# Scoring two neighbouring chunks back to back in batches 2 and 3 of a woven attention and MLP kernel

## The chip, the cores and the metric

The kernel runs on one core of a Trainium2 chip. The metric is the device time of one execution in microseconds (us), the median of several executions. TensorE is called PE here, VectorE DVE, ScalarE ACT, GpSimd POOL and SyncE SP, as the profile calls them.

## The reference, cut to what matters

Four batches, 8 heads, 768 positions, head size 64. A decaying linear attention, then a low-rank mixer over positions, then a two-layer MLP:

```python
for t in range(S):                      # attention, per batch and head
    state = gamma * state + outer(k[t], v[t])
    y[t] = scale * q[t] @ state
x = heads side by side of y             # (4, 768, 512)
u = x + (x.T @ U @ V).T                 # rank 32
out = u + relu(u @ w_ch1) @ w_ch2       # 512 -> 2048 -> 512
```

The kernel cuts the 768 positions into six chunks of 128. Within a chunk the attention is a masked score matrix (**score**, q times k, then **masking**), applied to v and added to q times the carried state (**mix**); **state** carries on to the next chunk.

## The kernel before: the parts that matter

PE works through the MLP of batch b-1, cut into pieces, and the attention of batch b is woven in between at marks, given as shares of that MLP's work. So "batch 2" below is the stretch in which the attention of batch 2 lies among the MLP pieces of batch 1. PSUM has eight banks, dealt out in rings:

```python
RINGS = {"mlp": [0, 1, 2], "s": [3, 4], "o": [5], "qk": [6], "st": [7],
         "A": [6, 0], "B": [1], "C": [2]}
...                                     # from batch 2 on: RINGS["mlp"] = [6, 0, 1, 2]

def score(b, ci):
    kT, qT = live["k", b, ci // 2][:, ci % 2], q_cols(b, ci)
    sp = [bank("s") for _ in range(2)]
    for h in range(H):                  # 8 matmuls of 64 rows
        r = ds(D * (h % 2), D)
        nc.tensor.matmul(sp[h % 2][:, ts(h // 2, P)], kT[r, h // 2],
                         qT[r, h // 2], start=True, stop=True)
    live["a", b, ci] = []
    for i in range(2):                  # 2 maskings on DVE
        a = rmid.tile([P, 4, P], bf16, tag=f"a{i}", bufs=2, ...)
        nc.vector.tensor_tensor(a, four(sp[i]), causal(mask), op=ALU.mult)
        live["a", b, ci].append(a)
```

`mix` fills bank "o" and ACT evacuates it. An MLP tile of the first layer fills a bank of the ring; its relu (one in three or four on DVE, the rest on ACT) writes `gT`. The second layer of batch 1 is done with seven products p1 to p7 where eight would be the plain way. Their inputs are sums `gS` that DVE makes; two of these come right after the last first-layer tile. p1 fills bank A, DVE reads it (`keep`, which writes `da`), and only then may p6 add into the same bank; p2 uses bank B, which is also a bank of the MLP ring:

```python
def p1(i): product("A", i, a11, w11, True);  keep("A", i, "a", i, 0)     # da
def p2(i): product("B", i, a12, w21, True);  give("B", i, i, 0, held["a", i])
def p6(i): product("A", i, s2, t2, False);   keep("A", i, "b", i, 1)
order = [(p1, 0), (p1, 1), (p2, 0), (p6, 0), (p6, 1), (p5, 0), ...]
```

POOL's preparation of batch 3's keys is held back by a small copy that reads the last `gT` of batch 1's MLP. At the end of each stretch `lr_turn` transposes `u` into `uT` by DMA, issued on SP, for the next MLP; finished output rows of batch 1 are stored by DMAs issued on ACT, later ones on SP.

## Time and profile before

| | before |
|---|---|
| time, median of the runs beside the changed kernel | 223.39 us (222.66 to 223.43) |
| span of the profiled execution | 220.9 us |
| PE / DVE / ACT / POOL busy | 96% / 66% / 41% / 38% |
| stretch of batch 2 | 44.13 us |
| stretch of batch 3 | 46.73 us |

The span is that of the instructions on the core; the time of the same execution is some 1.8 us longer. The stretches: the first starts where ACT evacuates the last part of batch 1's `uT` (87.82) and ends at the first MLP matmul on batch 2's `uT` (131.95); the second ends at the first MLP matmul on batch 3's (178.68). They leave out the start-up, where the same code takes 87.4 to 89.2 us from one fast trace to another, and the last part, 42.17 to 42.19 us in all twelve fast traces. How the rest of the page is read is told in the prediction below, with its lines.

### The profile page before, as it was taken

The page shows a single profiled execution, that of the slowest core. Times are in us where ns is not written, and L with a number is a line of the kernel's source. Part 1 is how long each engine was busy: PE and PEld are TensorE (multiplying, and loading weights), DVE is VectorE, ACT ScalarE, POOL GpSimd, SP SyncE. Part 2 cuts the span into 40 slices and gives each one's busy share as a digit, 9 for nine tenths or more (in the row PEclk, how much of TensorE's full clock was granted, in tenths as well). Part 3 has the DMA queues.
Part 4 walks back from the last instruction along what each step waited for, and adds up shares of the span by engine and source line. Part 5 has one row for each costly group of instructions (what it writes and reads, how often), then busy time and mean ns, then how long its engine had stood idle before and what let it go on. Part 6 is the DMA issues. An engine that isn't in the chain of part 4 may idle for free.

```text
span 220.9 us, 5520 instructions
## 1 busy us (share of the span) xinstructions
PE 213.1 (96%) x2235; PEld 147.5 (67%) x2235; DVE 146.6 (66%) x306; ACT 91.1 (41%) x187; POOL 83.0 (38%) x121
## 2 busy tenths in 40 slices
PE   6879999999999999999999999999999999999994
PEld 2568754596555554656778884756788856668884
DVE  7578666235775469698896856498868542867443
ACT  3347654475655314775712005767420035551000
POOL 5457869796978767000099900000000000000000
PEclk9999999999999999999999999999999999999999
DMA  6999899999999989999999587900001951000043
GB/s 169 301 293 298 279 356 246 326 380 223 230 235 239 244 195 236 178 324 254 214 238 202 140 186 188 129 0 3 1 3 48 155 205 23 4 0 0 11 158 119
DMA packets 84489, 38.82 MB, mean 176 GB/s; under 512 B 58384, under 2 KB 77552, under 8 KB 84464
## 3 DMA queue, kind: packets, MB, share of 16 engines
q1 hardware_dynamic: 83456, 36.84, 70.7%
q10 hardware_dynamic: 1008, 1.64, 2.2%
q8 instruction: 17, 0.28, 0.6%
q14 instruction: 8, 0.07, 0.1%
HBM read 27.46 MB, written 6.29 MB: 153 GB/s over the span
## 4 chain that ended last, share of the span: by engine, by line
PE 85%; DVE 8%; DMA 2%; ACT 2%; issue 1%; SPq 1%; DVEq 0%; ACTq 0%
PE mlp L755 35%; PE A L647 13%; PE mlp L803 8%; PE C L647 6%; PE B L647 3%; DVE a L512 3%; DMA in<-in_q_dram 2%; PE s L506 2%; DVE gS L600 2%; PE o L528 2%; ACT qT L85 2%; PE st L490 1%; PE mlp L193 1%; PE qk L465 1%; PE o L523 1%
## 5 line engine op out<-in xcount | busy, mean ns | idle before, releaser
L755 PE MATMUL mlp<-uT,w1b 128*128 128x512 f16 (+1 forms) x512 | 88.7, 326 | 0.2 <-DVE gT L760 0.2
L762 ACT ACTIVATE gT<-mlp 128x512 f16<-128x512 f32 (+1 forms) x94 | 45.3, 490 | 59.3 <-PE mlp L755 57.1
L755 PEld LDWEIGHTS <-w1b 128*128 128x128 f16 x512 | 48.3, 98 | 31.1 <-issue 0.3
L760 DVE TENSOR_SCALAR gT<-mlp 128x512 f16<-128x512 f32 (+1 forms) x34 | 18.9, 555 | 27.1 <-PE mlp L755 26.7
L647 PEld LDWEIGHTS <-gT 128*128 128x128 f16 x288 | 27.6, 98 | 3.5
L512 DVE TENSOR_TENSOR a<-s,mask 128x512 bf16<-128x512 f32 x36 | 23.1, 682 | 7.8 <-PE s L506 7.7
L803 PE MATMUL mlp<-w2b,gT 128*128 128x512 f16 x96 | 24.4, 380 | 0.0
L85 ACT ACTIVATE x<-o 128x512 f16<-128x512 f32 x20 | 11.9, 596 | 23.6 <-PE o L528 23.5
L306 POOL TENSOR_TENSOR kd<-in,gk 128x512 bf16<-128x512 f32 x18 | 19.2, 1074 | 5.1 <-DMA in<-in_k_dram 4.2
L647 PEld LDWEIGHTS <-gS 128*128 128x128 f16 x200 | 19.2, 98 | 2.6
L306 POOL TENSOR_TENSOR qd<-in,gq 128x512 bf16<-128x512 f32 x18 | 19.5, 1099 | 1.3 <-DMA in<-in_q_dram 1.2
L647 PE MATMUL A<-w2t,gT 128*128 128x256 f16 x144 | 18.2, 273 | 0.0
L85 ACT ACTIVATE state<-st 64x256 bf16<-64x256 f32 x40 | 15.0, 375 | 5.4 <-PE st L386 3.2
L803 PEld LDWEIGHTS <-gT 128*128 128x128 f16 x96 | 8.1, 98 | 6.9
L304 POOL CAST vd<-in 128x512 bf16<-128x512 f32 x18 | 11.5, 649 | 1.1 <-DMA in<-in_v_dram 0.9
L346 POOL CAST w2b<-in 128x512 f16<-128x512 f32 x16 | 9.6, 613 | 2.0 <-DMA in<-in_moe_w_ch_dram 1.3
L340 POOL CAST w1b<-in 128x512 f16<-128x512 f32 x16 | 9.4, 613 | 2.3 <-DMA in<-in_moe_w_ch_dram 1.9
L647 PE MATMUL B<-w2b,gT 128*128 128x256 f16 x72 | 9.3, 273 | 0.0
L647 PE MATMUL A<-w2t,gS 128*128 128x256 f16 x72 | 9.2, 273 | 0.0
L647 PE MATMUL A<-w2b,gT 128*128 128x256 f16 x72 | 9.0, 273 | 0.0
L565 DVE TENSOR_TENSOR x<-s,x 128x256 f16<-128x256 f32 (+1 forms) x16 | 8.1, 548 | 1.2 <-issue 0.7
L600 POOL COPY gate<-gT 128x1 f16<-128x1 f16 x1 | 0.2, 190 | 22.5 <-DVE gT L760 22.5
(147 smaller groups left out, 283.4 us busy)
## 6 DMA issues: line engine op xcount, KB each, us to landing
in<-in_moe_w_ch_dram SPq DMA_DIRECT2D x32, 256.0 KB, 5.6
in<-in_k_dram SPq DMA_DIRECT2D x24, 256.0 KB, 5.4
in<-in_q_dram SPq DMA_DIRECT2D x24, 256.0 KB, 4.7
in<-in_v_dram SPq DMA_DIRECT2D x24, 256.0 KB, 5.4
out_dram<-o SPq DMA_DIRECT2D x16, 256.0 KB, 2.2
out_dram<-o ACTq DMA_DIRECT2D x6, 256.0 KB, 2.4
out_dram<-o SPq DMA_DIRECT2D x3, 128.0 KB, 1.7
Uf<-in_moe_U_dram SPq DMA_DIRECT2D x1, 96.0 KB, 5.5
```

Of the source, the lines that this page charges most:

```text
L85: nc.scalar.activation(dst, src, AF.Copy)
L304: nc.gpsimd.tensor_copy(out=t, in_=src)
L306: nc.gpsimd.tensor_tensor(t, src, g, op=ALU.mult)
L340: nc.gpsimd.tensor_copy(out=w1b[:, c, ts(mb, 512)], in_=take("w1", mb, c))
L346: nc.gpsimd.tensor_copy(out=w2b[:, m], in_=take("w2", m))
L512: nc.vector.tensor_tensor(a, four(sp[i]), causal(mask), op=ALU.mult)
L565: nc.vector.tensor_tensor(us[b][:, ds(j0, nj), ts(c, P)], four(grown[b][c])[:, :nj], xs[b][:, ds(j0, nj), ts(c, P)], op=ALU.add)
L647: nc.tensor.matmul(acc[key, i], lhs[:, m, ts(i, P)], rhs[:, m], start=(fresh and m == 0), stop=(m == NH - 1), skip_group_check=True)
L755: nc.tensor.matmul(g_p[:, :sz], w1b[:, c, ts(m, P)], uTs[b][:, ds(j, nj), c], start=(c == 0), stop=(c == NCB - 1))
L760: nc.vector.tensor_relu(gT[:, m, ds(lo, sz)], g_p[:, :sz])
L762: nc.scalar.activation(gT[:, m, ds(lo, sz)], g_p[:, :sz], AF.Relu)
L803: nc.tensor.matmul(ch, gT[:, m, ts(j, P)], w2b[:, m], start=(m == 0), stop=(m == NM - 1))
```

## The change

The intent: PE loses time when it changes from 128-row matmuls to the 64-row ones of a score and back (a *mode change* below). So in batches 2 and 3 the scores of chunks ci+1 and ci are issued back to back. Each chunk's scores need two banks; the second chunk's take one bank of the MLP ring and the mix bank. The four maskings follow together, the next three MLP evacuations go to ACT, and all marks in batches 2 and 3 are set anew. Cut to its core:

```diff
-    def score(b, ci):
+    def score(b, ci, tags=("s", "s")):
...
-        sp = [bank("s") for _ in range(2)]
+        sp = [bank(t) for t in tags]
...
+    def screen(b, ci):                       # the maskings, split off
...
-            a = rmid.tile([P, 4, P], bf16, tag=f"a{i}", bufs=2,
+            a = rmid.tile([P, 4, P], bf16, tag=f"a{i}", bufs=3,
...
+    def score_two(b, ci):
+        score(b, ci + 1, ("mlp", "o"))
+        score(b, ci)
+        screen(b, ci + 1)
+        screen(b, ci)
+        spare[0] = 3 if b > 1 else 0
...
-                if n[0] % (3, 4, 4, 4)[b] == 0:
+                if spare[0]:
+                    spare[0] -= 1
+                    n[0] -= n[0] % (3, 4, 4, 4)[b] == 0
+                if n[0] % (3, 4, 4, 4)[b] == 0 and not spare[0]:
                     nc.vector.tensor_relu(gT[:, m, ds(lo, sz)], g_p[:, :sz])
...
+                two = [(0.255, 0.39, 0.52), (0.1, 0.27, 0.44)][b - 2]
...
+                if b > 1:
+                    p = two[i // 2]
+                    steps = [(state, p + (-0.035, 0.02)[i % 2]),
+                             (mix, p + (0.083, 0.108)[i % 2])]
+                    if i % 2 == 0:
+                        steps.append((score_two, p))
...
-            t = at[-1] + lag[2]
+            t = at[-1] + lag[2] if b == 1 else two[-1] + 0.108
```

More of the change, by code (lines that the diff above doesn't have):

```diff
@@ L507, in score @@
                              qT[r, h // 2], start=True, stop=True)
+        live["sp", b, ci] = sp
+    def screen(b, ci):
+        sp = live.pop(("sp", b, ci))
         live["a", b, ci] = []
         for i in range(2):
-            a = rmid.tile([P, 4, P], bf16, tag=f"a{i}", bufs=2,
+            a = rmid.tile([P, 4, P], bf16, tag=f"a{i}", bufs=3,
                           name=f"a{i}_{b}_{ci}")
@@ L513, in score, with score_one @@
             live["a", b, ci].append(a)
+    spare = [0]
+    def score_one(b, ci):
+        score(b, ci)
+        screen(b, ci)
+    def score_two(b, ci):
+        score(b, ci + 1, ("mlp", "o"))
+        score(b, ci)
+        screen(b, ci + 1)
+        screen(b, ci)
+        spare[0] = 3 if b > 1 else 0
     def mix(b, ci):
@@ L980 @@
                 for sc in range(NSC):
-                    d = at[2 * sc] - 0.05 if sc else at[0]
+                    d = two[sc] - (0.04, 0.05, 0.05)[sc]
                     tracks.append(([lambda b=b, sc=sc: q_order(
@@ L984 @@
             for i in range(NCK):
-                more = 0.012 if b == 1 and i in (0, 2) or b == 2 else 0.0
-                if b == 2 and i == 4:
-                    more = 0.022
-                for f, d in ((state, lag[0]), (score, lag[1]),
-                             (mix, lag[2] + more)):
-                    tracks.append(([part(f, b, i)], at[i] + d, at[i] + d))
-            t = at[-1] + lag[2]
+                more = 0.012 if b == 1 and i in (0, 2) else 0.0
+                if b > 1:
[4 more added lines that the diff above has]
+                        steps.append((score_two, p))
+                else:
+                    steps = [(state, at[i] + lag[0]),
+                             (score_one, at[i] + lag[1]),
+                             (mix, at[i] + lag[2] + more)]
+                for f, d in steps:
+                    tracks.append(([part(f, b, i)], d, d))
+            t = at[-1] + lag[2] if b == 1 else two[-1] + 0.108
             if b == 1:
```

## The prediction

> **What bounds the kernel now.** I read the page's busy shares and slices first. They say which engine to watch, and whether it has holes.
>
> ```profile
> PE 213.1 (96%) x2235; PEld 147.5 (67%) x2235; DVE 146.6 (66%) x306; ACT 91.1 (41%) x187; POOL 83.0 (38%) x121
> ...
> PE   6879999999999999999999999999999999999994
> ```
>
> TensorE (PE) is busy in 96% of the span, with full slices from the fourth to the last but one. So a change in the middle pays only by taking time out of PE's own stream: work, mode changes, or waits. Next I read PE in order of time, because 96% still hides small losses between matmuls. A place in batch 3 where a score (L506) stands alone in the MLP stream:
>
> ```profile
> 154.63 1.90 PE L755 MATMUL mlp<-uT,w1b 128*128 128x512 f16 x12
> 156.47 0.40 PE L506 MATMUL s<-qO,kT 64*128 64x128 bf16 x8
> 156.79 1.05 PE L755 MATMUL mlp<-uT,w1b 128*128 128x256 f16 x8
> 157.68 1.91 PE L647 MATMUL A<-w2b,gT 128*128 128x256 f16 x16
> ```
>
> The first column is the start. A 256-column matmul follows its neighbour after 0.109 us (eight in 157.68 - 156.79 = 0.89, and 0.87 elsewhere), a 512-column one after 0.216. The twelve in the first line are four wide and eight narrow: 4 x 0.216 + 8 x 0.109 = 1.74, but the score starts 1.84 after them: **0.10 us on entering**. The score's eight matmuls last 0.40 from first start to last end; less one duration of 0.216, seven steps take 0.18, so 0.026 each and 0.21 for eight. The next line comes 0.32 to 0.33 after: **0.11 us on leaving**. Both are inside "busy". One lone score thus costs 0.42 us, half of it for changing into 64-row mode and back.
>
> Then I looked for real waits, in the list of waits and in the stretch 109 to 115 us where slices of DVE (VectorE) and POOL meet:
>
> ```profile
> 109.50 0.42 DVE L760 TENSOR_SCALAR gT<-mlp 128x256 f16<-128x256 f32 x1 [0.51 <-PE mlp L755]
> 109.99 0.19 POOL L600 COPY gate<-gT 128x1 f16<-128x1 f16 x1 [22.49 <-DVE gT L760]
> 110.03 0.56 DVE L600 TENSOR_TENSOR gS<-gT 128x768 f16<-128x768 f16 x1
> ...
> 110.17 2.64 POOL L306 TENSOR_TENSOR kd<-in,gk 128x512 bf16<-128x512 f32 x2
> ...
> 110.62 1.28 DVE L600 TENSOR_TENSOR gS<-gS,gT 128x768 f16<-128x768 f16 x1
> ...
> 111.83 0.41 DVE L660 TENSOR_TENSOR da<-A,x 128x256 f32<-128x256 f32 x1
> ...
> 112.16 1.06 DVE L600 TENSOR_TENSOR gT<-gT 128x768 f16<-128x768 f16 x1
> ...
> 113.14 1.28 DVE L512 TENSOR_TENSOR a<-s,mask 128x512 bf16<-128x512 f32 x2
> ...
> 114.47 0.38 PE L506 MATMUL s<-qO,kT 64*128 64x128 bf16 x7 [0.39 <-DVE a L512]
> ```
>
> Here DVE runs without a hole and PE waits for it: the last score of batch 2 finds its second bank still being masked. PE's first score matmul is at 113.87 and the rest at 114.47, where 0.03 would do: 0.58 lost. The other wait for DVE in this batch is 0.16 at 101.43 (an MLP bank). Batch 3 shows no PE wait of note.
>
> **What the Trainium skill says.** "TensorEngine Tiling (Array Packing)", section Key Properties: "Changing tiling mode (not just tile) drains the TensorE". The trace agrees: the 0.10 and 0.11 above. "TensorE: Matmul & The Clock Gate", section The mechanism (Part 3): matmuls on different row groups run together; the trace has 0.026 us a step against 0.056 for 128 full rows (the 0.22 us of four L490). "SBUF — State Buffer", section Who interferes with whom: a VectorE instruction with two SBUF inputs contends with GpSimd reads, one with at most one does not. The trace agrees: gS (both inputs SBUF) is 0.56 before POOL starts and 1.28 beside it, while the masking (PSUM and SBUF) stays at 0.68 beside POOL at 113.14.
>
> **The change part by part.** The built order has the same 4472 PE rows, and one DVE row fewer.
> 1. *Fewer mode changes.* 12 lone scores in batches 2 and 3 become 6 double ones of sixteen matmuls: 6 x 0.21 = **-1.2 us**, all on PE's path.
> 2. *Old waits gone.* The second bank pair takes away the wait for a masked bank (-0.58) and, because the order moves, the 0.16 wait: **-0.7**.
> 3. *Four maskings in a row on DVE* (4 x 0.605 = 2.4 us; pitch from 113.14 to 114.34). In groups 1 and 2 of each batch three MLP tiles or more lie between a score and the first user of the borrowed MLP bank, over 1.7 us, and 3 to 4 us to the mix: hidden, but for about 0.15 in batch 3, where mix 2 comes 3.4 us after its score behind a late gS. `spare` sends the next three evacuations to ACT, which is idle 59% of the span.
> 4. *The mix bank as score bank.* A mix is evacuated by ACT: start 0.43 after the mix's eight matmuls begin (106.66 to 107.09), 0.60 long, so it is free 0.8 us after PE leaves it. New in batch 2: mixes 0 and 1 are parted only by a narrow tile and a state, 0.44 + 0.22 = 0.66: wait 0.2. Score 2 needs the reordered q that now stands behind four maskings, three gS and two more DVE instructions: by adding their pitches it is ready some 0.25 late. **+0.45**.
> 5. *Third group of batch 2.* The order is now: last MLP tile, double score, p1(0), p1(1), p2(0), p6(0). p6(0) adds into the bank that da must have read first, and DVE has the relu, two gS and **all four maskings** ahead of da. From the end of that tile: relu starts +0.20, gS +0.73, gS +1.32, held by POOL to +2.53, four maskings to +4.95, da done +5.36. PE has meanwhile only 0.10 + 0.43 + 0.11 + 3 x 0.873 = 3.26 us of work. So PE waits 2.1 us before p6(0) (part of it earlier, for the mix bank and for B's bank, which hide in the same chain): **+2.1**.
>
> Sum: -1.2 - 0.7 + 0.15 + 0.45 + 2.1 = **+0.8 us**; batch 3 gains 0.45, batch 2 loses 1.2. Nothing after batch 2's products depends on DVE closely, so I expect the loss to stay rather than be absorbed. The three timed runs spread over 222.66 to 223.43, and only one is near the profiled 222.64, so I take 223.1 as the honest start: 223.9.
>
> **Rivals.** (a) *Only the mode changes and old waits count* and DVE's queue has more slack than I add up: -1.2 - 0.7, hence about 221.5. For it: batch 3 has no POOL work and its DVE has holes of over 1 us. Against it: in batch 2 DVE was already the releaser. (b) *The borrowed banks starve the MLP ring*: each double score takes one of four MLP banks and the mix bank for up to 2 us; with ACT in arrears (relus, states and x in order), each of six groups could lose 0.3 to 0.5, about 225.5. Against it: three tiles take at least 1.3 us and ACT evacuates a narrow one in 0.38. (c) *Transfers gate the stage ends*: the earlier low-rank part issues its transposes earlier, and PE shows no wait at 131.95 where they are used, so this moves nothing.
>
> **Range and chances.** My estimate is 223.9. The step of 2.1 is the least sure: without POOL's hold it is 1.4, and the authors of such placements usually have tuned them, so I shade a little to 223.6. Range 222.0 to 225.0: from two thirds of rival (a) to most of (b). Two per cent is 4.5 us, more than all terms together on either side: faster 0.01, within 0.98, slower 0.01.
>
> **What would show it.** Right: six L506 groups of x16 in batches 2 and 3, lasting about 0.61 (15 x 0.026 + 0.216); PE entering each with a gap of 0.1; no L506 wait on the earlier masking; a PE wait of 1 to 2 us around p1 to p6 just after the third double score of batch 2 released by DVE, with four maskings side by side before da; batch 3 shorter by about 0.5. Wrong: if PE passes that place without a wait (then I am about 2 us too high), if x16 takes much longer than 0.61 (row mode across four banks not overlapping), or if relus on ACT hold MLP matmuls in several groups (too low).

## The result, and the profile after

| | before | after |
|---|---|---|
| time, median (lowest to highest) | 223.39 (222.66 to 223.43) | 224.15 (223.97 to 224.33) |
| ratio of mean fast times | | 1.0042 [1.0020, 1.0064] |
| stretch of batch 2 | 44.13 | 45.38 |
| stretch of batch 3 | 46.73 | 46.07 |

A ratio here and below is the mean time of one kernel's fast runs over that of the other's of the same rounds, so not quite the ratio of the medians. By the rule of 2% the two are the same; in the stretches the change costs 1.25 - 0.66 = 0.59 us. The rest of the 0.76 between the medians is within what the start-up does: that part was 0.86 us longer in the changed kernel's trace with the same code. 0.80 of it arises in the 16 warm-up matmuls, the last of which starts at 7.16 before and at 7.95 after. "TensorE: Matmul & The Clock Gate", section What's actually happening (Part 1), says that the window which decides on the clock runs freely and that the number of slow matmuls differs from run to run. These traces agree: of the 16, six took over 600 ns before and eleven after (medians 380 and 634 ns).

The page of the changed kernel, its busy times:

```profile
PE 213.0 (96%) x2235; PEld 148.1 (67%) x2235; DVE 144.8 (65%) x305; ACT 91.0 (41%) x188; POOL 82.1 (37%) x121
```

PE is as busy as before. What the change did has to be read in order of time. First a double score in batch 3, PE's timeline of the changed kernel (start, length, engine, line, operation):

```profile
136.87 1.89 PE L772 MATMUL mlp<-uT,w1b 128*128 128x512 f16 x8
138.69 0.23 PE L506 MATMUL mlp<-qO,kT 64*128 64x128 bf16 x1
...
138.93 0.39 PE L506 MATMUL s<-qO,kT 64*128 64x128 bf16 x8
139.25 1.04 PE L772 MATMUL mlp<-uT,w1b 128*128 128x512 f16 x4
```

Eight wide matmuls take 8 x 0.216 = 1.73, so PE would be ready at 138.60 and enters at 138.69: 0.09. From there to the next MLP matmul are 0.56 for sixteen matmuls: 16 x 0.026 is 0.42, and 0.14 on leaving. That is 0.65 for two chunks where two lone scores cost 2 x 0.42 = 0.84: **one mode change saved, 0.2 us**, as intended.

Then the third double score of batch 2, PE's timeline and then DVE's. A bracket is idle time and what ended it:

```profile
109.39 1.04 PE L772 MATMUL mlp<-uT,w1b 128*128 128x256 f16 x8
110.36 0.23 PE L506 MATMUL mlp<-qO,kT 64*128 64x128 bf16 x1
110.52 0.21 PE L506 MATMUL o<-qO,kT 64*128 64x128 bf16 x1
...
110.71 0.42 PE L506 MATMUL s<-qO,kT 64*128 64x128 bf16 x8
111.06 1.92 PE L664 MATMUL A<-w2b,gT 128*128 128x256 f16 x16
113.52 1.03 PE L664 MATMUL B<-w2b,gT 128*128 128x256 f16 x8 [0.55 <-DVE a L516]
115.65 1.03 PE L664 MATMUL A<-w2t,gS 128*128 128x256 f16 x8 [1.09 <-DVE da L677]
```

```profile
110.47 0.42 DVE L780 TENSOR_SCALAR gT<-mlp 128x256 f16<-128x256 f32 x1 [1.02 <-PE mlp L772]
111.00 0.56 DVE L617 TENSOR_TENSOR gS<-gT 128x768 f16<-128x768 f16 x1
111.59 1.28 DVE L617 TENSOR_TENSOR gS<-gS,gT 128x768 f16<-128x768 f16 x1
112.79 0.68 DVE L516 TENSOR_TENSOR a<-mlp,mask 128x512 bf16<-128x512 f32 x1
113.39 0.67 DVE L516 TENSOR_TENSOR a<-o,mask 128x512 bf16<-128x512 f32 x1
113.99 1.27 DVE L516 TENSOR_TENSOR a<-s,mask 128x512 bf16<-128x512 f32 x2
115.19 0.41 DVE L677 TENSOR_TENSOR da<-A,x 128x256 f32<-128x256 f32 x1
```

The borrowed mix bank comes free 0.14 late: the double score takes 0.70 from its first start to p1, where batch 3 has 0.56. PE goes on with both p1, and then it stands. Bank B is the MLP bank that the score borrowed, and it is free only after the masking of 112.79: p2 starts at 113.52 where 111.06 + 16 x 0.109 = 112.80 would do, 0.72 lost. p6 waits for `da`, which has stood behind all four maskings: it starts at 115.65 where p2's eight matmuls end their turn at 113.52 + 0.87 = 114.39, **1.26 lost**. In the kernel before, PE's timeline at the same place has no wait between these products, for the lone score put its two maskings into DVE later than `da`:

```profile
111.94 1.04 PE L647 MATMUL B<-w2b,gT 128*128 128x256 f16 x8
112.81 1.04 PE L647 MATMUL A<-w2t,gS 128*128 128x256 f16 x8
...
114.80 1.03 PE L647 MATMUL A<-w2t,gS 128*128 128x256 f16 x8
```

The last line comes after the lone score that the prediction shows waiting (113.87 and 114.47). It could have started at 112.81 + 0.87 + 0.42 = 114.10, so that old wait cost 0.70.

Note that the brackets show 0.55 and 1.09, less than the 0.72 and 1.26 that the starts give. A matmul's length in the trace reaches over its neighbour's start, so the idle time counts from an end that is later than PE's next possible start. Time lost on PE is read from starts. "Perfetto Trace Analysis", section Tensor Engine Instruction (MATMUL, LD_WEIGHTS), says that the profiler computes a matmul's end from its size instead of observing it; that agrees with the 0.17 between bracket and loss in both.

Last, a wait where the stretch of batch 2 ends. The changed kernel's PE, and below it the same place before:

```profile
133.57 0.21 PE L576 MATMUL st<-pc,V 32*128 32x128 f16 x1
134.06 2.75 PE L772 MATMUL mlp<-uT,w1b 128*128 128x512 f16 x12 [0.28 <-DVE o L685]
```

```profile
131.81 0.21 PE L559 MATMUL st<-pc,V 32*128 32x128 f16 x1
131.95 2.76 PE L755 MATMUL mlp<-uT,w1b 128*128 128x512 f16 x12
```

From the last low-rank matmul to the first of the MLP 0.14 us pass before and 0.49 after: 0.35 lost. The releaser named is DVE, but this matmul waits for several semaphores, among them those of the `uT` transposes, and the trace puts the wait down to the last one it saw. The experiments below settle which it was.

What batch 2 adds up to, every term read from starts:

| | us |
|---|---|
| three mode changes saved | -0.63 |
| old waits gone: MLP bank at 101.43 (0.32) and second score bank at 113.87 to 114.80 (0.70) | -1.02 |
| new: mix 1 waits for the mix bank 0.19, score 2 for the reordered q 0.21 | +0.40 |
| new: third double score, 0.14 for the mix bank, 0.72 for B, 1.26 for `da` | +2.12 |
| new: first MLP matmul waits for `uT` | +0.35 |
| sum (the stretches differ by 1.25) | +1.22 |

In batch 3 three mode changes are saved and nothing is lost: -0.63 by the sum, -0.66 by the stretches.

### The profile page after: what moved, and what is told of

Its sections match the earlier page's. It is cut to its first block, busy times and chain, and to the rows that moved or that the text cites. A ratio compares the mean times of both kernels' runs of the same rounds, so it can differ in the third digit from the quotient of the medians.

```text
span 222.3 us, 5518 instructions
## 1 busy us (share of the span) xinstructions
PE 213.0 (96%) x2235; PEld 148.1 (67%) x2235; DVE 144.8 (65%) x305; ACT 91.0 (41%) x188; POOL 82.1 (37%) x121
## 5 line engine op out<-in xcount | busy, mean ns | idle before, releaser
L782 ACT ACTIVATE gT<-mlp 128x512 f16<-128x512 f32 (+1 forms) x95 | 45.8, 492 | 67.0 <-PE mlp L772 48.8
L780 DVE TENSOR_SCALAR gT<-mlp 128x256 f16<-128x256 f32 (+1 forms) x33 | 18.3, 553 | 29.3 <-PE mlp L772 28.8
L306 POOL TENSOR_TENSOR qd<-in,gq 128x512 bf16<-128x512 f32 x18 | 18.8, 1060 | 1.1 <-DMA in<-in_q_dram 0.9
L516 DVE TENSOR_TENSOR a<-s,mask 128x512 bf16<-128x512 f32 x24 | 15.4, 682 | 5.5 <-PE s L506 5.5
```

Source lines behind the costliest of these rows:

```text
L306: nc.gpsimd.tensor_tensor(t, src, g, op=ALU.mult)
L780: nc.vector.tensor_relu(gT[:, m, ds(lo, sz)], g_p[:, :sz])
L782: nc.scalar.activation(gT[:, m, ds(lo, sz)], g_p[:, :sz], AF.Relu)
```

## The experiments

The theory: batch 3's gain is real; batch 2 loses because `da` and bank B stand behind four maskings in DVE's queue, made worse by POOL's work slowing `gS`; and there is a smaller loss at the transposes. Rivals: the borrowed banks starve the MLP ring everywhere; the mode change is no real cost; the wait before the next MLP is DVE's, as the trace labels it. All kernels gave correct results. The edits below are cut to their core. The experiments ran on three chips, and each ratio is taken against the kernel before on the same chip. One table for all; "stretches" is the sum of both stretches less that of before, "timed" is (ratio - 1) x 223.2 us:

| kernel | batch 2 | batch 3 | stretches | ratio, 95% interval | timed |
|---|---|---|---|---|---|
| before | 44.13 | 46.73 | | | |
| after | 45.38 | 46.07 | +0.59 | 1.0042 [1.0020, 1.0064] | +0.94 |
| after_again | 45.45 | 46.07 | +0.66 | 1.0029 [0.9997, 1.0062] | +0.65 |
| b3_only | - | - | - | 0.9966 [0.9935, 0.9998] | -0.76 |
| b2_only | 45.04 | 46.73 | +0.91 | 1.0026 [0.9993, 1.0059] | +0.58 |
| g3_single | 44.24 | 46.09 | -0.53 | 0.9986 [0.9947, 1.0024] | -0.31 |
| pool_late | 44.76 | 46.07 | -0.03 | 0.9988 [0.9951, 1.0025] | -0.27 |
| da_first | 44.90 | 46.07 | +0.11 | 1.0005 [0.9977, 1.0032] | +0.11 |
| stores_late | 45.03 | 46.09 | +0.26 | 1.0031 [0.9999, 1.0063] | +0.69 |
| stores_sync | 45.04 | 46.08 | +0.26 | 1.0011 [0.9989, 1.0033] | +0.25 |
| split | 45.36 | 46.88 | +1.38 | 1.0056 [1.0039, 1.0073] | +1.25 |
| best1 | 43.44 | 46.07 | -1.35 | 0.9940 [0.9907, 0.9974] | -1.34 |
| best2 | 42.90 | 46.08 | -1.88 | 0.9921 [0.9899, 0.9943] | -1.76 |

The batch 3 stretch of unchanged code repeats to 0.02 us from trace to trace, while the timed difference has an interval of some 0.4 to 0.9 us to either side. So the verdicts below rest on the stretches, and the times say whether they go the same way.

### b3_only and b2_only: one batch each

```diff
-                if b > 1:                       # in b3_only: old marks in batch 2
+                if b > 1 and b == 2:
+                    steps = [(state, at[i] + lag[0]), (score_one, at[i] + lag[1]), (mix, ...)]
+                elif b > 1:
```

b2_only is the same with `b == 3`.

> Double scores in batch 3 alone; batch 2 in the old order. Theory (six, here three, mode-change pairs of 0.21 us each are really saved, and the loss sits wholly in batch 2): 0.5 to 0.7 us faster than the kernel before; the stretch from the first MLP matmul of batch 2's tiles to that of batch 3's takes 46.1 us as in the changed kernel (46.7 before), and no PE wait for DVE da. Rival (borrowed banks or long DVE rows cost something everywhere): no faster than before, 0 to +0.4 us.

> Double scores in batch 2 alone; batch 3 in the old order. Theory: slower than the kernel before by 1.2 to 1.4 us (the changed kernel's loss without batch 3's gain), with PE waits of about 0.5 us at p2(0) and 1.1 us at p6(0) behind four maskings. Rival (the loss is a start-up effect of the profiled run, 0.8 us of slow clock in the first 9 us): about 0.2 us slower only.

b3_only: 222.44 us (median of the five fast runs, 221.91 to 222.97), 0.76 faster by the ratio, and the interval just leaves 1 out. Its profiled execution fell in the slow state (245.2 us of span at a lower clock), so its trace is not used. b2_only: +0.91 in the stretch, less than I had expected, and +0.58 timed. Its trace has both waits unchanged (0.54 and 1.09 in brackets); the one for `da` in PE's timeline:

```profile
116.17 1.03 PE L664 MATMUL A<-w2t,gS 128*128 128x256 f16 x8 [1.09 <-DVE da L677]
```

What is missing against the 1.25 is the wait for `uT`, which this trace doesn't have. So the change has a gain and a loss in different batches, and the ring of MLP banks does not starve in general: batch 3, with the same borrowed banks, shows no wait.

### g3_single: the third pair of batch 2 scored singly

```diff
-                if b > 1:
+                if b > 1 and (b == 2 and i // 2 == 2):
+                    steps = [(state, at[i] + lag[0]), (score_one, at[i] + lag[1]), (mix, ...)]
+                elif b > 1:
```

> As the changed kernel, but chunks 4 and 5 of batch 2 scored singly, at the old places; five double scores stay. Theory (the third double score of batch 2 costs 2.1 us of waits against 0.6 in the old order and one mode change): 1.2 to 1.7 us faster than the changed kernel, so 0.5 to 0.9 us faster than the kernel before; no PE wait at p6(0) for da, the old 0.6 us wait of the last single score back. Rival (the two other groups lose as much as they save, or the order of all six matters): at most 0.7 us faster than the changed kernel.

The stretch of batch 2 falls by 1.14 against after, to 0.11 above before. PE has no wait for `da` any more. But 0.35 of the 1.14 is the wait for `uT`, which this trace doesn't have either, as its first store leaves 2.8 us before the transposes again; the third pair itself accounts for some 0.8. That is less than the 2.12 of its waits, because a mode change comes back (0.21) and the new neighbours brought their own waits; PE's timeline:

```profile
111.29 1.03 PE L664 MATMUL A<-w2b,gT 128*128 128x256 f16 x8 [0.66 <-ACT gT L782]
...
115.71 0.38 PE L506 MATMUL s<-qO,kT 64*128 64x128 bf16 x7 [0.17 <-DVE a L516]
```

The first is p1 behind a relu on ACT that comes right before it (0.82 by the starts), the second the old wait for a masked score bank. The loss sits in the third pair, then, but going back to single scores there isn't the best cure.

### pool_late: POOL's preparation held until the last masking

```diff
     def mix(b, ci):
+        if b == 2 and ci == 4:
+            nc.gpsimd.tensor_copy(out=gate, in_=live["a", b, ci][1][:, 3, P - 1:])
```

> The changed kernel with POOL's preparation of batch 3 held by one small copy until the last masking of that group is done, so that DVE's second gS has no POOL work beside it. Theory (POOL's hold on DVE, 0.72 us, lies on the chain to da): that gS takes 0.56 instead of 1.28 us and p6(0) starts about 0.7 us earlier; 0.5 to 0.7 us faster than the changed kernel. Rival (gS is slow for another reason, its own operands): still 1.28 us, no change of the time; or POOL, four us later, holds up batch 3 and the time grows.

The second `gS` lasts 0.56 instead of 1.28, which agrees again with what the prediction cites on DVE and POOL reading SBUF together. DVE's line, and PE's next products:

```profile
110.81 0.56 DVE L619 TENSOR_TENSOR gS<-gS,gT 128x768 f16<-128x768 f16 x1
```

```profile
112.04 1.04 PE L666 MATMUL B<-w2b,gT 128*128 128x256 f16 x8
114.15 1.03 PE L666 MATMUL A<-w2t,gS 128*128 128x256 f16 x8 [1.06 <-DVE da L679]
```

The 0.72 saved in `gS` takes away the wait for B (0.72), and the stretch falls by 0.62; the wait for `uT` is there and takes 0.12 more than in after (132.06 to 132.67, less 0.14, is 0.47). The wait for `da` stays whole, since p2 now starts earlier by as much. So POOL's hold was a third of the loss in that group, and the four maskings ahead of `da` the larger part.

### da_first: two maskings before da, two after

```diff
+        if b == 2 and ci == 4:
+            score(b, ci + 1)
+            score(b, ci, ("mlp", "o"))
+            screen(b, ci)
+            spare[0] = 3
+            return
...
+                    elif b == 2 and i == 5:
+                        steps.append((screen, 0.56))
```

> The third double score of batch 2 stays double, but only the two maskings that free the MLP and mix banks stand ahead of da on DVE; the other two come after both da's. Theory (the four maskings are the term of 2.1 us): the sum of PE's waits at score, p2(0) and p6(0) falls from 2.1 to about 1.0 us, and batch 2's stretch from 45.4 to 44.1 to 44.4; 1.0 us faster than the changed kernel. Rival (the waits come from POOL's hold and the late start of that chain, not from the maskings' number): less than 0.5 us.

A half miss: p6 no longer waits, but the stretch falls by 0.48 only (45.38 to 44.90), which is just under the 0.5 that was put down for the rival. PE's timeline:

```profile
113.86 1.03 PE L670 MATMUL B<-w2b,gT 128*128 128x256 f16 x8 [0.69 <-DVE a L516]
114.80 1.03 PE L670 MATMUL A<-w2t,gS 128*128 128x256 f16 x8
...
118.10 0.29 PE L551 MATMUL o<-vd,a 128*128 128x64 bf16 x4 [0.31 <-DVE a L516]
```

The wait for B stays, and the one for `da` was turned into one of mix 5 for the last maskings, which DVE begins at 116.77. They stand behind two more sums, 0.86 and 1.06 long beside POOL, where the same two take 0.55 each in best2 with POOL held. By the starts mix 5 loses 0.77: its second half begins at 118.10, where the four matmuls of L546 from 117.00 and four of L551 would have let it begin at 117.33. So order alone isn't the cure while POOL slows DVE's queue: the rival is right in that POOL's hold keeps the chain late, and the theory in that `da` waited behind the maskings.

### stores_late and stores_sync: the wait before the next MLP

The changed schedule issues the `uT` transposes earlier, so they now go out beside the six stores of 256 KB that wait on ACT. First I tried to hold the stores back in program order:

```diff
-            for _ in range(0 if keep else late):
+            for _ in range(0 if keep or at < total * hold else late):     # hold = 0.80 in batch 2
```

> The changed kernel with the output stores of batch 1 held until four fifths of that stretch, so that they do not share the DMA engines with the low-rank transposes. Theory (the 0.3 to 0.4 us wait before batch 2's first MLP matmul is the second transpose, landing after 7.6 us beside the stores instead of 5.3): the transposes land within 5.5 us, that wait is gone, batch 2's stretch shrinks by 0.35. Rival (the wait is for DVE, as the profile's label says): it stays 0.3.

A miss: the stores still left at 124.76, as ACT had nothing in its stream between the old and the new place. By chance this trace shows no wait (0.14 from the last low-rank matmul to the MLP), so it decides nothing by itself. Then the same (that hold included) with the stores on SP's queue, behind the transposes:

```diff
-                stores.append((nc.sync if b > 1 else nc.scalar,
+                stores.append((nc.sync,
```

> The changed kernel with batch 1's output stores put on SyncE's queue behind the two low-rank transposes (the last attempt left them where they were). Theory (the wait before batch 2's first MLP matmul is the second transpose sharing the DMA engines with the stores): both transposes land within 5.5 us, no PE wait there, batch 2's stretch 45.0 instead of 45.4. Rival (the transposes are slow by themselves or the wait is DVE's): landing still over 7 us, the wait stays 0.3 to 0.4.

The DMAs between 121 and 134 us in the timeline of before, after and stores_sync (start, length of the whole row, issuing queue):

```profile
122.17 10.46 ACTq L607 DMA_DIRECT2D out_dram<-o  x6
125.07 9.80 SPq L592 DMA_TRANSPOSE uT<-x  x3
```

```profile
124.98 3.88 SPq L609 DMA_TRANSPOSE uT<-x  x2
125.19 8.33 ACTq L624 DMA_DIRECT2D out_dram<-o  x5
```

```profile
124.83 2.74 SPq L609 DMA_TRANSPOSE uT<-x  x2
127.66 6.57 SPq L624 DMA_DIRECT2D out_dram<-o  x6
```

And how long the transposes of `uT` took to land, for after and for stores_sync:

```profile
DMA to landing us min/median/max: 3.2/5.6/7.6
```

```profile
DMA to landing us min/median/max: 3.2/4.1/4.6
```

In stores_sync the wait is gone and the stretch is 0.34 shorter than after's. One trace alone could be chance, as stores_late shows. But the trace settles the wait directly. In after, the second transpose of `uT` lands at 133.93 and the matmul starts at 134.06; in the four other traces with the wait the matmul also follows that landing by 0.14. And it does not need the DVE instruction that the label names: in stores_sync it starts while that one still runs (DVE, then PE):

```profile
133.45 0.42 DVE L685 TENSOR_TENSOR o<-C,db 128x256 f32<-128x256 f32 x1 [0.45 <-PE C L664]
133.57 2.76 PE L772 MATMUL mlp<-uT,w1b 128*128 128x512 f16 x12
```

That the stores slow the transposes is seen over the twelve fast traces: where the slowest transpose took 7.6 or 7.7 us (after, after_again, pool_late, da_first, best1) PE waits for `uT`; where it took 7.3 or less (stores_late 7.3, b2_only 6.8, split 6.2, before and g3_single 5.3, best2 4.9, stores_sync 4.6) it doesn't. Before and g3_single send the first stores ahead of the transposes, best2 and stores_sync send all of them behind; in the other eight the first store leaves 0.2 us after the first transpose, and the slowest transpose takes 6.2 to 7.7. So the 0.35 is not a fixed cost of the change: five of these eight traces have the wait, and three do not. "DMA: Bandwidth & Descriptors", section Rules for kernel authors, says that the DMAs of different issuing engines run on the same 16 DMA engines and interleave; the landing times here agree.

### split: a mode change put back between the two scores

```diff
+        if split:
+            nc.tensor.matmul(sp[0][:, :P], ident, ident, start=True, stop=True,
+                             skip_group_check=True)
```

One full 128-row matmul between the scores of each pair; its output is overwritten by the second score.

> The changed kernel with one full-row 128x128 matmul put between the two scores of each pair (its output is overwritten), so that the array leaves 64-row mode and comes back: the mode change by itself. Theory (0.21 us for each way out and in, and 0.056 for the matmul): batch 3's stretch grows by 3 x 0.27 = 0.8 us to 46.9; batch 2's by 0.5 (two of three, the third hidden in the wait for DVE). Rival (mode changes cost nothing by themselves, the gaps are waits for the LDWEIGHTS or for banks): batch 3's stretch grows by 3 x 0.06 = 0.2 us or less.

The stretch of batch 3 grows from 46.07 to 46.88, by 0.81, that is 0.27 a pair. PE's timeline of a pair in batch 3:

```profile
138.34 0.22 PE L509 MATMUL o<-qO,kT 64*128 64x128 bf16 x1
138.48 0.23 PE L505 MATMUL s<-ident 128*128 128x128 bf16 x1
138.65 0.40 PE L509 MATMUL s<-qO,kT 64*128 64x128 bf16 x8
```

0.14 from the last 64-row matmul to the full one and 0.17 from there to the next 64-row one are 0.31, where the changed kernel has 0.05 between its two scores (138.88 to 138.93): 0.26 more. Less 0.056 for the full matmul itself, 0.20 is the change there and back, as the prediction had it. The weight load that comes with it is no rival: every matmul in these traces has one (2235 of both on the page), and those of L490 still follow each other after 0.055. In batch 2, whose stretch without the wait for `uT` is 45.03 (45.38 - 0.35), it adds only 0.33 for three pairs instead of the expected 0.5: where PE waits for DVE or for q afterwards, work put in before the wait is free.

### after_again: the changed kernel once more

> The changed kernel once more, for a like-for-like comparison on the chip of the experiments. Theory (a fixed loss in batch 2 of 0.9 to 1.25 us and a fixed gain in batch 3 of 0.66 us): batch 2's stretch 45.0 to 45.4 us and batch 3's 46.1 us in the trace, and 0.3 to 0.8 us slower than the kernel before. Rival (the first result was mostly the start-up's slow clock): stretches nearer to 44.1 and 46.7, and no difference in the median.

+0.66 in the stretches and +0.65 timed, so the +0.94 of the first comparison holds some start-up.

### best1 and best2: all cures together

best1 has da_first, the hold of stores_late, a POOL copy that waits for the last masking of chunk 5, and some marks shifted (mix 1 at +0.118, the q order 0.04 earlier). best2 has in addition the stores on SP behind the transposes; mix 1 is back at +0.108 and q is ordered at -0.195:

```diff
+        if (b, ci) == (2, 5):                    # in screen
+            nc.gpsimd.tensor_copy(out=gate, in_=a[:, 3, P - 1:])
...
+        if b == 2 and ci == 4:                   # in score_two: as in da_first
...
-                stores.append((nc.sync if b > 1 else nc.scalar,
+                stores.append((nc.sync,
...
-                        steps.append((0.57 + 0.08 * sc,
+                        steps.append((0.58 + 0.08 * sc,
...
-                    d = two[sc] - (0.04, 0.05, 0.05)[sc]
+                    d = two[sc] - (0.04, 0.195 if b == 2 else 0.05, 0.05)[sc]
```

> All remedies together: two maskings ahead of da, POOL held until the group's last masking, stores late, mix 1 one tile later, the reordered q of chunks 2 and 3 earlier. Theory (all five waits are separate and the double scores' saving of 1.2 us is real): batch 2's stretch 42.5 to 43.0 us (44.1 before), batch 3's 46.1 (46.7), 1.7 to 2.2 us faster than the kernel before. Rival (taking one wait away uncovers another in the same chain): batch 2's stretch not under 43.5.

> The version with all remedies, now with the stores really behind the transposes, mix 1 back at its place and the reordered q of chunks 2 and 3 made before batch 2's first score, where DVE has a hole. Theory: batch 2's stretch 42.8 to 43.2 us (43.44 in the first such version), batch 3's 46.1; 1.9 to 2.3 us faster than the kernel before. Rival (the stores delay the later transposes of batch 3, or the q comes too early and DVE waits for its transpose): no better than the first version's 1.7.

best1: 221.62 us (220.92 to 222.85) beside 223.36 of before. The stretch of batch 2 is 43.44, a miss against the expected 42.5 to 43.0: the wait for `uT` is still there (0.39), and the shifted marks of mix 1 and q turned their waits into one of 0.33 for an MLP bank. best2: **221.05 us** (220.83 to 222.34) beside 223.11, faster than both kernels, by 0.8% against the one before (by the rule of 2% all kernels here are the same), with 42.90 for batch 2 as expected; the 1.76 timed is a little under the 1.9 to 2.3 expected. In its timelines `da` comes after two maskings, and PE runs through almost without a wait (p2 is 0.14 late after 110.06 + 1.75); DVE, then PE:

```profile
112.41 0.41 DVE L685 TENSOR_TENSOR da<-A,x 128x256 f32<-128x256 f32 x1
```

```profile
111.95 1.03 PE L672 MATMUL B<-w2b,gT 128*128 128x256 f16 x8
112.87 1.03 PE L672 MATMUL A<-w2t,gS 128*128 128x256 f16 x8
```

## Why the prediction was right, and where it was not

The predicted time was 223.6, within 2%; measured were 224.15 and, again, 223.82. That it would stay within 2% was hardly in doubt, as all terms together are smaller; what counts is the sum and its terms. The sum before shading was +0.8; the stretches show +0.59 and +0.66.

1. *Fewer mode changes*, -1.2: right. Batch 3 fell by 0.66 with three of them, and split puts 0.27 a pair back.
2. *Old waits gone*, -0.7: right in kind, too small. They were 0.32 and 0.70. I took the 0.16 from the bracket of the trace, where the starts give 101.43 - (99.80 + 12 x 0.109) = 0.32; and for the score bank I took 0.58 between its two lines, where the product after it starts at 114.80 instead of 114.10.
3. *Four maskings hidden*, but for 0.15 in batch 3: the 0.15 did not come; batch 3 has no wait at all.
4. *Mix bank and q*, +0.45: measured 0.19 and 0.21.
5. *Third group*, +2.1: the best of the terms. From the end of the last tile to p6 I had added up 5.36; the trace has 5.39 (110.26 to 115.65), and the chain in DVE is the one named. b2_only shows it alone and da_first and best2 take it apart.

**Rival (c) was dismissed wrongly.** "This moves nothing" was argued from the kernel before, where PE shows no wait at the end of the stretch. But there the first store left 2.9 us before the transposes; in the changed kernel the stores start beside them, the slowest transpose takes 7.6 us instead of 5.3, and PE loses 0.35. I looked at whether the transposes were early, not at what they would share the DMA engines with. The undersized step 2 and this made up for each other: -0.3 and +0.35. That was luck, the more so as the second is not in every trace.

The shading by 0.3 for "usually tuned" rested on no trace, and the runs don't tell whether it helped: as a difference, +0.5 with it and +0.8 without lie on either side of the +0.59 and +0.66. The absolute 223.6 is 0.55 under the first median because the start was taken as 223.1 where the median beside it was 223.39. Rival (b) was rightly set aside, with batch 3 as the evidence. One line was misread: the prediction calls the first `gS` (0.56) one "before POOL starts", but it runs from 110.03 to 110.59 and POOL's work begins at 110.17. It only started earlier; the clean comparison is pool_late, where the second one has no POOL work beside it and takes 0.56 too. The "4472 PE rows" stand in no trace: the pages have 2235 matmuls and 2235 weight loads, before and after. What is left open: the part of the differences in time beyond the stretches, up to 0.4 us, is only argued to be the start-up clock, as no run controlled it. The count of slow warm-up matmuls doesn't order the start-ups either: da_first, with eight, took 89.03, and g3_single, with eleven, 88.88.

## What to carry to other kernels

Grouping work on the bound engine saves its mode changes, but it also bunches the work that follows on another engine: before you group, add up that engine's queue ahead of the very instruction that the bound engine waits for next, and put that one first. Measure a change of half a per cent in stretches of the trace that leave out the start-up, and read losses from starts and not from idle times. When a schedule moves a transfer, ask which other transfers it will now meet.

## What the Trainium skill lacked or had wrong

- "TensorEngine Tiling (Array Packing)", section Key Properties, gives no size for the drain of a mode change. Here it is 0.09 to 0.10 us from full to 64-row mode and 0.11 to 0.14 back; with a full matmul put between two scores, 0.27 us a pair with that matmul.
- "DMA: Bandwidth & Descriptors", section Rules for kernel authors, has no figure for a transpose beside plain stores. The slowest transpose of `uT` landed after 6.2 to 7.7 us in the eight traces where six stores of 256 KB start beside it, and after 4.6 and 4.9 in the two where they come behind it.
- "Perfetto Trace Analysis", section Tensor Engine Instruction (MATMUL, LD_WEIGHTS), doesn't say what an estimated end does to idle times: the waits that the trace shows as 0.16, 0.55 and 1.09 us cost 0.32, 0.72 and 1.26 by the starts.
